# Layer one in a hand-written TensorE order: feed-forward products in quarter parts, attention steps as whole groups between them

## The chip, the cores and the metric

The kernel runs on one core of a Trainium2 chip. The metric is the device time of one launch in microseconds (us); lower is better. A core has five engines with a queue of their own: TensorE (PE, matrix products; PEld is its weight load), VectorE (DVE), ScalarE (ACT), GpSimd (POOL) and SyncE (SP, which issues DMA transfers). They meet only at semaphores.

## The reference

Windowed attention (each position sees itself and the 63 before it), then two feed-forward layers, all in float32:

```python
# q, k, v: (4, 8, 576, 64), window 64
scores = scale * np.matmul(q, k.transpose(0, 1, 3, 2))
scores = np.where(mask, scores, -1000000000.0)
scores = scores - np.max(scores, axis=-1, keepdims=True)
attn = np.exp(scores)
attn = attn / (np.sum(attn, axis=-1, keepdims=True) + 1e-09)
attn_out = np.matmul(attn, v)
x = attn_out.transpose(0, 2, 1, 3).reshape(2304, 512)
# layer one: w_in (512, 2048), w_out (2048, 512)
h = x @ w_in; r = np.maximum(h, 0.0); g = r * r; y1 = g @ w_out
# layer two: same sizes, elu
h = y1 @ w_in2; g = np.where(h > 0.0, h, np.exp(np.minimum(h, 0.0)) - 1.0)
y2 = g @ w_out2
```

## The kernel before

**Products.** A feed-forward product is made of three matmuls on pairs of a rounded high part and a low remainder: high by high, high by low, low by high (`mm3`, L454). A column tile of 512 tokens is one PSUM bank.

**Layer one.** The tokens are cut into blocks of 512, 256, 512, 512 and 512. Blocks t = 0, 1 and 2 run through the plain layer; blocks 3 and 4 meet it in another form, with combined weights (`stepw`, L692, from block 2's last steps on). A block has 16 steps j. A step makes one hidden tile: `m_h` issues 12 matmuls into the PSUM tile `ph` (4 chunks of the contraction by 3); ACT then makes relu and square into `g` and the high part of `gs`, DVE the low part. `m_out` multiplies `gs` into four accumulators o0 to o3 (4 by 3 matmuls; in a trace `o`). The loop issues h two steps ahead of o, and there are three buffers for `gs`. In block 0 `ph` has two banks, after that one.

**Attention.** A unit is one pair of heads for one block; the units of a block must be done before its h starts, so they are placed in the steps of the block ahead; those of blocks 3 and 4 (eight units, `pairs`) in block 2. A unit is

- `u_S` (L366): score matmuls, 64x128, two heads (a = 0, 1) on two halves of the array and in two PSUM banks; 16 of them for a block of 512, 8 for 256;
- softmax: per 128 columns one DVE maximum (`nm`, with the mask), one ACT exponential with its sum, a DVE normalisation in `pb`;
- `u_T` (L406): 8 transposes of `pb` through the identity, 4 to a PSUM bank, each bank copied by ACT to an SBUF tile `pt`;
- `u_PV` (L420): 16 matmuls of 64 columns on `pt` and the values; `u_X` copies the result (`xs`, or `xr` for the pairs, from which ACT makes `xo`).

`pa` is the PSUM tile of these, from three banks; `pt` shares its four SBUF buffers with `ev`, the copy of a finished accumulator that a DMA stores to `x2d`. `u_V2` does transposes and products of two units at once.

**What sets the order.** The program is written step by step, but inside layer one nothing pins the order on PE: a scheduler with a model of the engines places each instruction, and within a step's reach it takes h, o and attention matmuls as their inputs come. Two tools pin order: `slot` hangs background work (decoding and combining weights, with its ACT, DVE and DMA instructions: `top`, `tl`, `wo`, `y`) behind the last ACT and DVE instruction; and `in_turn`, used before only behind layer one, issues a function and chains its PE instructions (`last["pe"]`) behind the previous ones. It chains PE alone; ACT, DVE and SP stay with the scheduler, and each engine works its queue in order.

Of the kernel before, what the change touches and what calls it, by code (L numbers as in the profile page):

```python
# [19 lines left out]
P = 128  # L20
# [6 lines left out]
def window_attention_then_two_mlps(  # L27
# [86 lines left out]
    def split(hi, lo, x, eng):  # L114

        last["hi"] = act.activation(out=hi, in_=x, func=AF.Copy)
        last["lo"] = eng.tensor_tensor(out=lo, in0=x, in1=hi.bitcast(F32), op=ALU.subtract)
# [235 lines left out]
    def u_S(u, alloc):  # L353
        t, p = u
        qr, kr = raw[u]["q"], raw[u]["k"]
        m = BLOCKS[t] // P
        nm = at.tile([P, 2 * NQ], F32, tag="nm", name="nm")
        sm = at.tile([P, 2 * NQ], F32, tag="sm", name="sm")
        rc = at.tile([P, 2 * NQ], F32, tag="rc", name="rc")
        pss = [alloc() for _ in range(2)]  # L360
        for i in range(m):
            for a in range(2):
                d = slice(a * D, (a + 1) * D)
                for c in range(2):
                    o = (2 * i + c) * WIN
                    nc.tensor.matmul(  # L366
                        out=pss[a][c * WIN:(c + 1) * WIN, i * P:(i + 1) * P],
                        lhsT=qr[d, o:o + WIN], rhs=kr[d, o:o + P], start=True, stop=True,
                    )
        prb[u] = []  # L370
        for a0, heads in ((0, 1), (1, 1)) if m == NQ else ((0, 2),):
            w = heads * m
            pb = at.tile([P, 4 * P], F32, tag="pb", name="pb", bufs=4)
            for i in range(w):
                a, g = a0 + i // m, i % m
                b = a * m + g
                c, z = slice(i * P, (i + 1) * P), slice(g * P, (g + 1) * P)
                lead = [(T0[t] + (2 * g + h) * WIN) % S == 0 for h in range(2)]
                vec.tensor_tensor_reduce(
                    out=pb[:, c], in0=pss[a][:, z], in1=mask[1 + lead.index(True) if any(lead) else 0],  # L380
                    scale=-SCALE, scalar=3.0e38, op0=ALU.add, op1=ALU.min,
                    accum_out=nm[:, b:b + 1],
                )
                last["act"] = act.activation(
                    out=pb[:, c], in_=pb[:, c], func=AF.Exp,
                    bias=nm[:, b:b + 1], scale=-1.0, accum_out=sm[:, b:b + 1],
                )
            b0 = a0 * m
            r = rc[:, b0:b0 + w]
            vec.tensor_scalar(  # L390
                out=r, in0=sm[:, b0:b0 + w], scalar1=1.0e-9, scalar2=None, op0=ALU.add
            )
            vec.reciprocal(out=r, in_=r)
            x = pb[:, :w * P].rearrange("p (b x) -> p b x", x=P)
            last["dve"] = vec.tensor_tensor(
                out=x, in0=x, in1=r.unsqueeze(2).broadcast_to([P, w, P]), op=ALU.mult
            )
            prb[u].append((pb, w))

    def u_T(u, alloc):  # L400

        pts = []
        for pb, w in prb.pop(u):
            ps = alloc()
            for i in range(0, w * P, P):
                nc.tensor.transpose(out=ps[:, i:i + P], in_=pb[:, i:i + P], identity=ident)  # L406
            pt = at.tile([P, 512], F32, tag="pt", name="pt", bufs=4)
            copy(pt[:, :w * P], ps[:, :w * P], act)
            pts += [pt[:, i:i + P] for i in range(0, w * P, P)]
        return pts  # L410

    def u_PV(u, pts, alloc):
        t, p = u
        vr = raw.pop(u)["v"]
        ps = alloc()
        m = BLOCKS[t] // P
        for b in range(2 * m):
            for a in range(2):
                d = slice(a * D, (a + 1) * D)
                nc.tensor.matmul(  # L420
                    out=ps[d, b * WIN:(b + 1) * WIN], lhsT=vr[:, b % 2, b // 2, d],
                    rhs=pts[a * m + b // 2][:, (b % 2) * WIN:(b % 2 + 1) * WIN], start=True, stop=True,
                )
        return ps

    def u_X(u, ps):
        t, p = u
        n = BLOCKS[t]
        if t > TW:
            k = p // 2, t - TW - 1  # L430
            if k not in XQ:
                XQ[k] = xp.tile([P, CH, NMAX], F32, tag=f"xs{2 * k[0] + k[1]}", name="xr")
            copy(XQ[k][:, p % 2], ps[:, :n], vec if p % 2 else act)
            return
        s = xs[t, p] = xp.tile([P, 2, NMAX], F32R, tag=f"xs{p}", name="xs")
        split(s[:, 0, :n], s[:, 1, :n], ps[:, :n], vec)
# [1 line left out]
    def u_V(u, alloc):  # L438
        u_X(u, u_PV(u, u_T(u, alloc), alloc))

    def u_V2(us, alloc):

        pts = [u_T(u, alloc) for u in us]
        pss = [u_PV(u, x, alloc) for u, x in zip(us, pts)]
        for u, ps in zip(us, pss):
            u_X(u, ps)

    gs = {}
    acc = {}
# [5 lines left out]
                out=ps, lhsT=a[x], rhs=b[y], start=(first and i == 0), stop=(final and i == 2)  # L455
            )

    def m_h(t, j):
        n = BLOCKS[t]
        w = wt[j, 0]  # L460
        ps = h_alloc(t)
        for c in range(KD):
            x = xs[t, c]
            mm3(
                ps[:, :n],
                [w[:, r, c * P:(c + 1) * P] for r in range(2)],
                [x[:, r, :n] for r in range(2)],
                c == 0, c == KD - 1,
            )
        g = sc.tile([P, NMAX], F32, tag="g", name="g")  # L470
        s = sc.tile([P, 2, NMAX], F32R, tag="gs", name="gs", bufs=GB)
        act.activation(out=g[:, :n], in_=ps[:, :n], func=AF.Relu)
        act.activation(out=g[:, :n], in_=g[:, :n], func=AF.Square)
        split(s[:, 0, :n], s[:, 1, :n], g[:, :n], vec)
        gs[t, j] = s

    def m_out(t, j):
        n = BLOCKS[t]
        w = wt[j, 1]
        g = gs.pop((t, j))  # L480
        if j == 0:
            acc[0] = [ps_o.tile([P, 512], F32, tag=f"o{m}", name=f"o{m}") for m in range(KD)]
        for m, ps in enumerate(acc[0]):
            mm3(
                ps[:, :n],
                [w[:, r, m * P:(m + 1) * P] for r in range(2)],
                [g[:, r, :n] for r in range(2)],
                j == 0, j == NJ - 1,
            )
        if j == NJ - 1:  # L490
            leave1(t)

    def leave1(t):
        n = BLOCKS[t]
# [8 lines left out]
    def load_to(i):  # L503
        while nxt[0] <= min(i, len(order) - 1):
            u_load(order[nxt[0]])
            nxt[0] += 1
# [28 lines left out]
    def h_alloc(t):  # L535
        return among((0, 1) if t == 0 else (0,), "ph")
# [392 lines left out]
    lwx = ctx.enter_context(ExitStack())  # L929
    pairs = [(t, p) for t in range(TW + 1, NB) for p in range(HP)]  # L930
    for i, (t, j) in enumerate(its):
        if t == 0 and j > 2 and j % 2:
            m_out(t, j - 1)
            m_out(t, j)
        for n in ([i + LA] if t or j < 2 else [i + LA - 1, i + LA] if j % 2 else []):
            if n < len(its):
                m_h(*its[n])
        if t == 0 and j < 2:
            m_out(t, j)
        if (t, j) == (1, 0):  # L940
            late[0] = 1
        if (t, j) == (TW, 0):
            hw += [wts.tile([P, 2, NMAX], F32R, tag=f"w{k}", name="tl") for k in range(2)]
            more_lanes(0, 1)
        i0 = i - NJ * TW + 2
        if i0 in (2, 4, 6, 8):
            u_V2(pairs[i0 - 2:i0], a_alloc)
        if 0 <= i0 < len(pairs):
            u = pairs[i0]
            load_to(order.index(u) + 1)  # L950
            u_S(u, a_alloc)
        if t < TW:
            p, r = divmod(j, 3)
            u = (t + 1, p)
            if p < HP and r == 0:
                load_to(order.index(u) + 1)
                u_S(u, a_alloc)
            elif p < HP and r == 2 and p % 2:
                u_V2([(t + 1, p - 1), u], a_alloc)
        else:  # L960
            if j == 7:
                att.close()
                lw.append(pool(lwx, "lw", 1))
                w0_load(10)
            if j == 4:
                xw = x_make(-1, NMAX)
                next(xw)
            if j in (8, 9):
                next(xw)
            if j == 14:  # L970
                tl.update({k: lw[0].tile([P, NMAX], F32, tag=f"tl{k}", name="tl") for k in (1, 6, 7)})
            if j > 13:
                stepw(0, j - 13)
        if t:
            m_out(t, j)
        if t == 0:
            decode(min(LA + 3 + j, NU))
        slot(SLOTS.get((t, j), 0))
# [175 lines left out]
```

## Time and profile before

| | us |
|---|---|
| median of 3 runs (837.52 to 840.39) | 839.19 |
| profiled execution, its own time | 837.73 |
| its span in the trace | 836.0 |
| PE busy | 816.8 (98%) |
| DVE busy | 590.6 (71%) |
| ACT busy | 553.0 (66%) |
| mean granted PE clock | 0.996 |

1.7 us of the profiled execution lie outside its span. A row of the trace's timeline is a run of like instructions; its duration is that of the run with the pipeline's end, which overlaps the next row, so what a run cost PE is the distance from its start to the start of the next. The trace counts the float32 attention matmuls of 64 and 128 columns of `u_S` and `u_PV` twice: x32 there are 16 instructions. Stretches of the span by time: block 0's steps about 45 to 130 us, block 1's to 207, block 2's to about 315 (with the pairs' attention up to 284), combined steps from there on.

### The profile page before, as it was taken

What the parts mean: (1) busy time and instruction counts of PE and PEld (TensorE: products, weight loads), DVE (VectorE), ACT (ScalarE), POOL (GpSimd) and SP (SyncE); (2) the same over time, 40 slices, a digit from 0 to 9 for tenths busy, and PEclk for the clock granted to TensorE, in tenths of its full rate; (3) what the DMA queues carried; (4) which work ended last, traced back from release to release, by engine and by line L of the source; (5) the groups of instructions that cost most, each with busy time, mean ns of one, the idle gap of its engine ahead of it and who ended that gap; (6) DMA issues with size and microseconds to landing.
All of it is one profiled execution on the core that took longest, in us unless ns stands there. A gap on an engine that the chain in (4) does not pass through costs nothing.

```text
span 836.0 us, 14761 instructions
## 1 busy us (share of the span) xinstructions
PE 816.8 (98%) x5196; PEld 734.7 (88%) x5196; DVE 590.6 (71%) x1372; ACT 553.0 (66%) x1278; POOL 5.0 (1%) x23
## 2 busy tenths in 40 slices
PE   4899999999999999999999999999999999999998
PEld 3687788998777788888878899999999999999998
DVE  6898616877577857665675756698676798566875
ACT  5776536677777768777884557667477766477552
POOL 2000000000000000000000000000000000000000
PEclk9899999999999999999999999999999999999999
DMA  9996214556476498999969697878977876877832
GB/s 355 416 405 216 78 65 154 201 183 213 149 253 229 153 337 305 396 330 323 340 245 327 226 319 286 300 267 277 316 259 266 323 257 211 284 266 276 300 119 57
DMA packets 98681, 214.85 MB, mean 257 GB/s; under 512 B 26544, under 2 KB 53680, under 8 KB 90160
## 3 DMA queue, kind: packets, MB, share of 16 engines
q1 hardware_dynamic: 97776, 213.72, 72.8%
q8 instruction: 41, 0.67, 0.3%
q14 instruction: 32, 0.26, 0.1%
q10 hardware_dynamic: 832, 0.20, 0.1%
HBM read 160.41 MB, written 53.48 MB: 256 GB/s over the span
## 4 chain that ended last, share of the span: by engine, by line
PE 91%; ACT 5%; DMA 2%; DVE 1%; issue 1%; SPq 0%; ACTq 0%
PE o L454 23%; PE po L890 20%; PE px L692 14%; PE ph L454 12%; PE py L692 10%; PE po L692 6%; ACT pb L54 3%; PE pa L420 2%; PE pa L366 2%; PE pa L406 1%; PE px L890 1%; DMA tl<-in_moe_w_in_dram 1%; DMA wd<-wo 0%; DMA wraw<-in_moe_w_in_dram 0%; ACT top L54 0%
## 5 line engine op out<-in xcount | busy, mean ns | idle before, releaser
L454 PE MATMUL o<-gs,w 128*128 128x512 f32 (+1 forms) x960 | 216.4, 372 | 0.8 <-ACT gs L54 0.7
L454 PEld LDWEIGHTS o<-gs,w 128*128 128x128 f32 x960 | 167.1, 188 | 33.9 <-issue 2.2
L890 PE MATMUL po<-g,wr 128*128 128x384 f32 (+1 forms) x972 | 168.6, 333 | 0.0
L890 PEld LDWEIGHTS po<-g,wr 128*128 128x128 f32 x972 | 167.5, 188 | 0.0
L454 PE MATMUL ph<-xs,w 128*128 128x512 f32 (+1 forms) x576 | 126.0, 362 | 1.9 <-ACT xs L54 1.7
L54 ACT ACTIVATE g<-gr 128x384 fp32r<-128x384 f32 x168 | 86.9, 524 | 55.5 <-PE po L890 49.1
L454 PEld LDWEIGHTS ph<-xs,w 128*128 128x128 f32 x576 | 94.9, 189 | 19.2 <-ACT xs L54 2.6
L54 DVE TENSOR_TENSOR g<-gr,g 128x384 fp32r<-128x384 f32 x168 | 89.9, 552 | 16.1 <-ACT g L54 15.1
L692 PE MATMUL px<-xo,wr 128*128 128x384 f32 x432 | 83.8, 334 | 0.0
L692 PEld LDWEIGHTS px<-xo,wr 128*128 128x128 f32 x432 | 75.8, 188 | 0.3
L54 DVE TENSOR_TENSOR gs<-g,gs 128x512 fp32r<-128x512 f32 (+1 forms) x64 | 39.8, 622 | 42.1 <-ACT gs L54 41.6
L54 ACT ACTIVATE pb<-pb,nm 128x128 f32<-128x128 f32 x144 | 55.8, 389 | 14.9 <-DVE nm L54 14.9
L54 ACT ACTIVATE sy<-px 128x384 f32<-128x384 f32 x69 | 33.8, 490 | 41.7 <-PE px L692 41.3
L692 PE MATMUL po<-xo,wr 128*128 128x384 f32 x288 | 56.2, 334 | 0.0
L692 PE MATMUL py<-xo,wr 128*128 128x384 f32 x288 | 55.7, 334 | 0.0
L54 ACT ACTIVATE g<-ph 128x512 f32<-128x512 f32 (+1 forms) x48 | 24.9, 518 | 45.0 <-PE ph L454 44.9
L54 DVE TENSOR_TENSOR gr<-gr 128x384 f32<-128x384 f32 x96 | 52.2, 553 | 0.5
L54 DVE TENSOR_TENSOR gr<-sy,py 128x384 f32<-128x384 f32 x48 | 26.6, 554 | 35.1 <-PE py L692 23.3
L692 PEld LDWEIGHTS po<-xo,wr 128*128 128x128 f32 x288 | 50.5, 188 | 0.0
L692 PEld LDWEIGHTS py<-xo,wr 128*128 128x128 f32 x288 | 50.5, 188 | 0.0
L692 PE MATMUL px<-xo,w 128*128 128x512 f32 x192 | 46.4, 389 | 0.0
L54 DVE TENSOR_TENSOR wo<-y,wo 128x256 fp32r<-128x256 f32 (+1 forms) x65 | 32.2, 508 | 19.3 <-ACT wo L54 18.5
(88 smaller groups left out, 1098.1 us busy)
## 6 DMA issues: line engine op xcount, KB each, us to landing
wr<-wd SPq DMA_DIRECT2D x66, 1024.0 KB, 6.4
wd<-wo SPq DMA_DIRECT2D x38, 512.0 KB, 4.9
wr<-wd SPq DMA_DIRECT2D x24, 768.0 KB, 5.0
w<-wd SPq DMA_DIRECT2D x56, 256.0 KB, 5.6
vr<-in_v_dram SPq DMA_DIRECT2D x16, 512.0 KB, 5.6
wraw<-in_moe_w_in_dram SPq DMA_DIRECT2D x16, 511.8 KB, 8.7
wraw<-in_moe_w_out_dram SPq DMA_DIRECT2D x16, 511.8 KB, 9.8
wd<-tl SPq DMA_DIRECT2D x15, 512.0 KB, 4.6
```

The lines of the kernel that those rows point to most:

```text
L54: r = fn(*a, **kw)
L366: nc.tensor.matmul(out=pss[a][c * WIN:(c + 1) * WIN, i * P:(i + 1) * P], lhsT=qr[d, o:o + WIN], rhs=kr[d, o:o + P], start=True, stop=True,)
L406: nc.tensor.transpose(out=ps[:, i:i + P], in_=pb[:, i:i + P], identity=ident)
L420: nc.tensor.matmul(out=ps[d, b * WIN:(b + 1) * WIN], lhsT=vr[:, b % 2, b // 2, d], rhs=pts[a * m + b // 2][:, (b % 2) * WIN:(b % 2 + 1) * ...
L454: last["pe"] = nc.tensor.matmul(out=ps, lhsT=a[x], rhs=b[y], start=(first and i == 0), stop=(final and i == 2))
L692: last["pe"] = nc.tensor.matmul(out=ps[:, :NH], lhsT=w[:, wr_, c * P:(c + 1) * P], rhs=x[:, xr_, c], start=first and n == 0, stop=final an ...
L890: last["pe"] = nc.tensor.matmul(out=ps[m][:, lo:hi], lhsT=w[:, y, m * P:(m + 1) * P], rhs=s[:, x, lo:hi], start=k in fresh and p == 0 and ...
```

## The change

`m_h` and `m_out` become lists of four parts of three matmuls each (`parts_h`: one per chunk c; `parts_out`: one per accumulator m). Scores and the halves of `u_V2` (now `parts_V`: transposes of one unit, transposes of the other, products of one, products of the other) become items `between`. `mesh` puts each item ahead of an equal share of the step's parts, and issues all of it through `in_turn`, so that PE keeps the order as written: within a step h, then o. The score matmuls, the transposes and the products now set `last["pe"]`. In block 1 the scores move from j = 0, 3, 6, 9 to 0, 2, 6, 8. Of the pairs, an even score is put behind its step (`after_`) and the odd one at the front of the next step. For t = 1 and 2, o is now issued ahead of the step's other work.

```diff
@@ u_S
-                    nc.tensor.matmul(
+                    last["pe"] = nc.tensor.matmul(
@@ u_V2
-    def u_V2(us, alloc):
-        pts = [u_T(u, alloc) for u in us]
-        pss = [u_PV(u, x, alloc) for u, x in zip(us, pts)]
-        for u, ps in zip(us, pss):
-            u_X(u, ps)
+    def parts_V(us, alloc):
+        pts = {}
+        def turn(u):
+            pts[u] = u_T(u, alloc)
+        def close(u):
+            u_X(u, u_PV(u, pts.pop(u), alloc))
+        return [(f, u) for f in (turn, close) for u in us]
@@ m_h, m_out
-    def m_h(t, j):
+    def parts_h(t, j):
...
+        def piece(c):
...
+        return [(piece, c) for c in range(KD)]
...
-    def m_out(t, j):
+    def parts_out(t, j):
...
+        return [(piece, m) for m in range(KD)]
+
+    def mesh(fill, between):
+        if between:
+            gap = len(fill) // len(between)
+            fill = [x for k, b in enumerate(between) for x in [b] + fill[k * gap:(k + 1) * gap]] + fill[len(between) * gap:]
+        for f, a in fill:
+            in_turn(f, a)
@@ the loop over steps
+        fill, between, after_ = [], [], []
         if t == 0 and j > 2 and j % 2:
-            m_out(t, j - 1)
-            m_out(t, j)
+            fill += parts_out(t, j - 1) + parts_out(t, j)
...
-                m_h(*its[n])
+                fill += parts_h(*its[n])
+        if t or j < 2:
+            fill += parts_out(t, j)
...
         if t < TW:
-            p, r = divmod(j, 3)
-            u = (t + 1, p)
-            if p < HP and r == 0:
-                load_to(order.index(u) + 1)
-                u_S(u, a_alloc)
-            elif p < HP and r == 2 and p % 2:
-                u_V2([(t + 1, p - 1), u], a_alloc)
+            u = {x: (t + 1, p) for p, x in enumerate(((0, 3, 6, 9), (0, 2, 6, 8))[t])}.get(j)
+            ready_ = {5: 0, 11: 2}.get(j)
+            if ready_ is not None:
+                between += parts_V([(t + 1, ready_ + r) for r in range(2)], a_alloc)
+            if u:
+                between.append((score, u))
+        if i0 in (2, 4, 6, 8):
+            between += parts_V(pairs[i0 - 2:i0], a_alloc)
+        if 0 <= i0 < len(pairs):
+            (between if i0 < 2 or i0 % 2 else after_).append((score, pairs[i0]))
+        mesh(fill, between)
+        mesh(after_, [])
...
-        if t:
-            m_out(t, j)
```

Three places show what this makes of the queues. L454 of before is L458 of after; 128x256 are block 1's columns, 128x512 those of blocks 0 and 2.

PE in block 1, at the transposes and products of its first two units, before:

```order
L406 MATMUL pa<-ident,pb 128x128 x4
L454 MATMUL ph<-xs,w 128x256 x12
L406 MATMUL pa<-ident,pb 128x128 x4
L420 MATMUL pa<-pt,vr 64x64 x14
L454 MATMUL o_1500<-gs,w 128x256
L454 MATMUL o_1501<-gs,w 128x256
L454 MATMUL o_1502<-gs,w 128x256
L454 MATMUL o_1503<-gs,w 128x256
L420 MATMUL pa<-pt,vr 64x64
L454 MATMUL ph<-xs,w 128x256 x12
```

And the same place after:

```order
L406 MATMUL pa<-ident,pb 128x128 x8
L458 MATMUL ph<-xs,w 128x256 x6
L406 MATMUL pa<-ident,pb 128x128 x8
L458 MATMUL ph<-xs,w 128x256 x6
L420 MATMUL pa<-pt,vr 64x64 x16
L458 MATMUL o_1500<-gs,w 128x256 x3
L458 MATMUL o_1501<-gs,w 128x256 x3
L420 MATMUL pa<-pt,vr 64x64 x16
L458 MATMUL o_1502<-gs,w 128x256 x3
L458 MATMUL o_1503<-gs,w 128x256 x3
```

Transposes in fours and products in broken groups have become groups of 8 and 16, one unit each, with half an h or half an o between two.

PE in block 2, from the end of one pair's products through the next pair's scores, before (o_2631 to o_2634 are block 2's accumulators):

```order
L420 MATMUL pa<-pt,vr 64x64 x15
L366 MATMUL pa<-kr,qd 64x128 x16
L454 MATMUL ph<-xs,w 128x512 x2
L454 MATMUL o_2631<-gs,w 128x512 x2
L366 MATMUL pa<-kr,qd 64x128 x8
L454 MATMUL o_2631<-gs,w 128x512
L454 MATMUL o_2632<-gs,w 128x512 x3
L454 MATMUL o_2633<-gs,w 128x512 x2
L366 MATMUL pa<-kr,qd 64x128 x8
L454 MATMUL o_2633<-gs,w 128x512
```

And after (the accumulators are o_2562 to o_2565 there):

```order
L420 MATMUL pa<-pt,vr 64x64 x16
L458 MATMUL o_2564<-gs,w 128x512 x3
L458 MATMUL o_2565<-gs,w 128x512 x3
L366 MATMUL pa<-kr,qd 64x128 x32
L458 MATMUL ph<-xs,w 128x512 x12
L458 MATMUL o_2562<-gs,w 128x512 x3
```

The first score of a pair was whole and the second in two halves, each between products; now both stand in one row of 32 with a whole h behind them.

PE where block 1 ends, before (o_1501 to o_1503 are block 1's last products, o_2631 and on block 2's first):

```order
L454 MATMUL ph<-xs,w 128x512 x12
L454 MATMUL o_1501<-gs,w 128x256 x2
L454 MATMUL o_1502<-gs,w 128x256 x3
L454 MATMUL o_1503<-gs,w 128x256 x3
L406 MATMUL pa<-ident,pb 128x128 x8
L454 MATMUL o_2631<-gs,w 128x512 x3
L406 MATMUL pa<-ident,pb 128x128 x4
L454 MATMUL o_2632<-gs,w 128x512 x3
L454 MATMUL ph<-xs,w 128x512 x12
L454 MATMUL o_2633<-gs,w 128x512 x3
L454 MATMUL o_2634<-gs,w 128x512 x3
L406 MATMUL pa<-ident,pb 128x128 x4
```

And after:

```order
L458 MATMUL ph<-xs,w 128x512 x12
L458 MATMUL o_1500<-gs,w 128x256 x3
L458 MATMUL o_1501<-gs,w 128x256 x3
L458 MATMUL o_1502<-gs,w 128x256 x3
L458 MATMUL o_1503<-gs,w 128x256 x3
L406 MATMUL pa<-ident,pb 128x128 x8
L458 MATMUL ph<-xs,w 128x512 x6
L406 MATMUL pa<-ident,pb 128x128 x8
L458 MATMUL ph<-xs,w 128x512 x6
L420 MATMUL pa<-pt,vr 64x64 x16
L458 MATMUL o_2562<-gs,w 128x512 x3
L458 MATMUL o_2563<-gs,w 128x512 x3
```

The second unit's transposes stood behind 18 products of block 2, and the last four of them behind a whole h; now six matmuls of h stand between the two units' groups.

Over the whole of layer one PE has 834 such rows in place of 1005. The transposes of block 2's units, in block 1's steps, fall into 4 groups (9 before) and those of the pairs into 8 (14); the products into 4 (8) and 8 (7), and those in block 0's steps into 4 (3); the scores into 4 (11) for block 2's units and 5 (12) for the pairs, whose first two stand in block 1's last steps. The two heads alternate through the whole score in 8 of these 12 scores; in one of block 2's units and in the second score of three of the four pairs, one head's 8 come first and then the other's.

ACT's queue at the second pair, between the pair's exponentials and the copies of its transposes, before (`xo` belongs to the pair before, `top`, `wo` and `tl` to the combined weights):

```order
L54 ACTIVATE pb,sm<-pb,nm 128x128 x7
L54 ACTIVATE gs<-g 128x512
L54 ACTIVATE pb,sm<-pb,nm 128x128
L54 ACTIVATE top<-tl 128x256
L54 ACTIVATE wo<-y 128x2x256
L54 ACTIVATE g<-ph 128x512
L54 ACTIVATE top<-top 128x256
L54 ACTIVATE pt<-pa 128x512
```

And after:

```order
L54 ACTIVATE pb,sm<-pb,nm 128x128 x8
L54 ACTIVATE g<-ph 128x512
L54 ACTIVATE xo<-xr 128x1024
L54 ACTIVATE top<-tl 128x256
L54 ACTIVATE wo<-y 128x2x256
L54 ACTIVATE top<-top 128x256
L54 ACTIVATE g<-g 128x512
L54 ACTIVATE pt<-pa 128x512 x3
```

`xo` has moved from the midst of the exponentials behind them, and a relu's square now stands ahead of three copies.

## Rows read from the trace of the kernel before

**Rows 1.** The page's first part: busy time and share of each engine.

```profile
PE 816.8 (98%) x5196; PEld 734.7 (88%) x5196; DVE 590.6 (71%) x1372; ACT 553.0 (66%) x1278; POOL 5.0 (1%) x23
```

**Rows 2.** Waits of PE: who for whom: total us, times, longest us.

```profile
PE pa L420 <- ACT pt L54: 2.5, 3, 1.7
```

**Rows 3.** Busy time by stretch: span, PE, PEld, DVE, ACT, POOL, clock, DMA share, GB/s.

```profile
140.00:200.00 60.00, 60.00 (x631) 55.21 (x626) 48.36 (x156) 42.10 (x139) 0.00 (x0) 1.00 0.56 186
200.00:284.00 84.00, 82.78 (x787) 66.79 (x786) 59.60 (x220) 66.10 (x204) 0.00 (x0) 1.00 0.63 216
...
315.00:420.00 105.00, 105.00 (x465) 86.95 (x464) 69.10 (x149) 81.35 (x175) 0.00 (x0) 1.00 0.95 341
```

**Rows 4.** Timeline of PE in block 0: start us, us, engine, line, operation, count.

```profile
107.93 2.88 PE L454 MATMUL o<-gs,w 128*128 128x512 f32 x12
110.65 2.89 PE L454 MATMUL ph<-xs,w 128*128 128x512 f32 x12
113.38 1.04 PE L406 MATMUL pa<-ident,pb 128*128 128x128 f32 x8
114.17 3.00 PE L454 MATMUL o<-gs,w 128*128 128x512 f32 x12
117.00 1.97 PE L454 MATMUL ph<-xs,w 128*128 128x512 f32 x8
118.91 1.15 PE L420 MATMUL pa<-pt,vr 128*64 128x64 f32 x32
119.99 3.02 PE L454 MATMUL o<-gs,w 128*128 128x512 f32 x12
122.84 3.79 PE L454 MATMUL ph<-xs,w 128*128 128x512 f32 x16
```

**Rows 5.** Timeline of PE in block 1: scores' first and last piece, half products.

```profile
126.56 1.08 PE L366 MATMUL pa<-kr,qd 64*64 64x128 f32 x14
...
160.16 0.69 PE L420 MATMUL pa<-pt,vr 128*64 128x64 f32 x16
160.77 1.69 PE L454 MATMUL ph<-xs,w 128*128 128x256 f32 x12
...
175.09 0.44 PE L366 MATMUL pa<-kr,qd 64*64 64x128 f32 x4
```

**Rows 6.** Timeline of PE in block 2: two pairs' first score, the later one's second.

```profile
218.11 1.10 PE L366 MATMUL pa<-kr,qd 64*64 64x128 f32 x32
...
240.05 1.10 PE L366 MATMUL pa<-kr,qd 64*64 64x128 f32 x32
241.08 0.50 PE L454 MATMUL ph<-xs,w 128*128 128x512 f32 x1
...
242.66 1.09 PE L366 MATMUL pa<-kr,qd 64*64 64x128 f32 x16
243.69 1.21 PE L454 MATMUL o<-gs,w 128*128 128x512 f32 x4
244.83 1.09 PE L366 MATMUL pa<-kr,qd 64*64 64x128 f32 x16
```

**Rows 7.** Timeline of ACT; in brackets idle time before and its releaser.

```profile
147.19 0.36 ACT L54 ACTIVATE g<-ph 128x256 f32<-128x256 f32 x1
...
210.05 0.60 ACT L54 ACTIVATE pt<-pa 128x512 f32<-128x512 f32 x1 [1.35 <-DMA x2d<-ev]
...
242.78 1.04 ACT L54 ACTIVATE xo<-xr 128x1024 fp32r<-128x1024 f32 x1
244.12 0.39 ACT L54 ACTIVATE pb<-pb,nm 128x128 f32<-128x128 f32 x1
```

**Rows 8.** Timeline of DVE: low part of `gs`, and one maximum of a score.

```profile
110.08 0.69 DVE L54 TENSOR_TENSOR gs<-g,gs 128x512 fp32r<-128x512 f32 x1 [3.75 <-ACT gs L54]
...
241.19 0.29 DVE L54 CUSTOM_DVE_ANT_0 pb<-pa,mask 128x128 f32<-128x128 f32 x1
```

**Rows 9.** The tile `ev` between 200 and 225 us: issue to landing.

```profile
DMA to landing us min/median/max: 2.7/3.8/4.7
```

More of the change, by code (lines that the diff above doesn't have):

```diff
@@ L405, in u_T @@
             for i in range(0, w * P, P):
-                nc.tensor.transpose(out=ps[:, i:i + P], in_=pb[:, i:i + P], identity=ident)
+                last["pe"] = nc.tensor.transpose(out=ps[:, i:i + P], in_=pb[:, i:i + P], identity=ident)
             pt = at.tile([P, 512], F32, tag="pt", name="pt", bufs=4)
@@ L419, in u_PV @@
                 d = slice(a * D, (a + 1) * D)
-                nc.tensor.matmul(
+                last["pe"] = nc.tensor.matmul(
                     out=ps[d, b * WIN:(b + 1) * WIN], lhsT=vr[:, b % 2, b // 2, d],
@@ L456, in mm3 @@
             )
-    def m_h(t, j):
+    def parts_h(t, j):
         n = BLOCKS[t]
[L460 to L463, printed above, removed]
+        ps = []
+        def piece(c):
+            if c == 0:
+                ps.append(h_alloc(t))
+            w, x = wt[j, 0], xs[t, c]
             mm3(
-                ps[:, :n],
+                ps[0][:, :n],
                 [w[:, r, c * P:(c + 1) * P] for r in range(2)],
@@ L469, in m_h, with piece @@
             )
[L470 to L475, printed above, removed]
-    def m_out(t, j):
-        n = BLOCKS[t]
[L479 to L483, printed above, removed]
+            if c < KD - 1:
+                return
+            g = sc.tile([P, NMAX], F32, tag="g", name="g")
+            s = sc.tile([P, 2, NMAX], F32R, tag="gs", name="gs", bufs=GB)
+            act.activation(out=g[:, :n], in_=ps[0][:, :n], func=AF.Relu)
+            act.activation(out=g[:, :n], in_=g[:, :n], func=AF.Square)
+            split(s[:, 0, :n], s[:, 1, :n], g[:, :n], vec)
+            gs[t, j] = s
+        return [(piece, c) for c in range(KD)]
+    def m_h(t, j):
+        for f, c in parts_h(t, j):
+            f(c)
+    def parts_out(t, j):
+        n = BLOCKS[t]
+        def piece(m):
+            w, g = wt[j, 1], gs[t, j]
+            if j == 0 and m == 0:
+                acc[0] = [ps_o.tile([P, 512], F32, tag=f"o{k}", name=f"o{k}") for k in range(KD)]
             mm3(
-                ps[:, :n],
+                acc[0][m][:, :n],
                 [w[:, r, m * P:(m + 1) * P] for r in range(2)],
@@ L489, in m_out @@
             )
-        if j == NJ - 1:
-            leave1(t)
+            if m == KD - 1:
+                gs.pop((t, j))
+                if j == NJ - 1:
+                    leave1(t)
+        return [(piece, m) for m in range(KD)]
[5 more added lines that the diff above has]
+            in_turn(f, a)
     def leave1(t):
@@ L931, in window_attention_then_two_mlps @@
     for i, (t, j) in enumerate(its):
+        fill, between, after_ = [], [], []
         if t == 0 and j > 2 and j % 2:
-            m_out(t, j - 1)
-            m_out(t, j)
+            fill += parts_out(t, j - 1) + parts_out(t, j)
         for n in ([i + LA] if t or j < 2 else [i + LA - 1, i + LA] if j % 2 else []):
             if n < len(its):
-                m_h(*its[n])
-        if t == 0 and j < 2:
-            m_out(t, j)
+                fill += parts_h(*its[n])
+        if t or j < 2:
+            fill += parts_out(t, j)
         if (t, j) == (1, 0):
@@ L944, in window_attention_then_two_mlps, with score @@
             more_lanes(0, 1)
[L945 to L949, printed above, removed]
+        def score(u):
             load_to(order.index(u) + 1)
             u_S(u, a_alloc)
+        i0 = i - NJ * TW + 2
         if t < TW:
-            p, r = divmod(j, 3)
-            u = (t + 1, p)
-            if p < HP and r == 0:
-                load_to(order.index(u) + 1)
-                u_S(u, a_alloc)
-            elif p < HP and r == 2 and p % 2:
-                u_V2([(t + 1, p - 1), u], a_alloc)
-        else:
+            u = {x: (t + 1, p) for p, x in enumerate(((0, 3, 6, 9), (0, 2, 6, 8))[t])}.get(j)
[10 more added lines that the diff above has]
+        mesh(after_, [])
+        if t == TW:
             if j == 7:
@@ L973, in window_attention_then_two_mlps @@
                 stepw(0, j - 13)
-        if t:
-            m_out(t, j)
         if t == 0:
```

## The prediction

> **What bounds the kernel now.** I read the engines' shares first: PE is busy for 816.8 of 836.0 us, DVE and ACT for 71% and 66% [rows 1]. So PE's queue sets the end, and an edit can gain only by making its matmuls shorter, by taking away what one kind of matmul costs behind another, or by removing idle time. The stretches come second. From 140 to 200 us PE has no idle time, and from 200 to 284 us it lacks 1.22 us [rows 3]; in the list of waits the largest entry that falls into layer one is products that wait for ACT's copies of transposes, 2.5 us in three times [rows 2]. In that stretch ACT is busy for 66.1 of 84 us [rows 3]: not the bound, but the engine with least to spare. Third, PE's timeline, read from start to start, which shows what a switch costs.
>
> A plain run of 12 matmuls of 512 columns takes 2.72 us (107.93 to 110.65), 0.227 each. The run of 12 behind the transposes takes 2.83 (114.17 to 117.00), the 8 ahead of a unit's products 1.91 where 8 by 0.227 make 1.81, and the 12 behind them 2.85 [rows 4]. So an attention group costs 0.11 us beside itself if it is transposes, and 0.10 + 0.13 = 0.23 if it is products. For scores: 4 matmuls between two groups take 1.14 (243.69 to 244.83) where 0.91 would do: 0.23 again [rows 6].
>
> The scores hold the larger surprise. A whole score of 16 matmuls takes 1.03 us (240.05 to 241.08), and half a score, 8 matmuls, takes as long (242.66 to 243.69) [rows 6]. In the whole one the two heads alternate, on two halves of the array; in the half one a single head's 8 stand alone. Splitting a score by heads doubles its price.
>
> **The change, part by part.** The sum goes against the profiled execution's 837.73 us; its median stands 1.46 us above that, and I carry the difference over.
>
> *Scores whole, not split.* Block 2's four scores lie in 11 pieces from 126.56 to 175.09 [rows 5], whose own times, start to start, add to 7.3 us. After, three are whole and one in halves by head: 3 x 1.03 + 2.05 = 5.1. Gain 2.2. Of the pairs, the first score becomes whole (0.35 gained); the second ones of three pairs stay in halves, so nothing is gained inside these.
>
> *Score groups joined.* 11 groups become 4, and 12 become 5: 14 groups fewer at 0.22: gain 3.1.
>
> *Products of attention.* Half a unit's products take 0.61 us (160.16 to 160.77) [rows 5], a whole unit's 1.08 [rows 4]; a group more costs 0.61 x 2 + 0.23 - 1.08, about 0.35. Block 1's steps have 4 groups fewer, block 0's one more, the pairs one more of which the parts were unequal (taken at nothing, 0.35 at most): gain 1.0.
>
> *Transposes.* 5 and 6 groups fewer at up to 0.11: between 0 and 1.2; since some switches are now between transposes and products with no feed-forward run between, I take 0.5.
>
> *Idle time that goes.* The 1.22 us of block 2's stretch [rows 3] were waits of an order that is no more: gain 1.2, and the new order's waits are charged below.
>
> Gains together: 2.2 + 0.35 + 3.1 + 1.0 + 0.5 + 1.2 = 8.35, between 6 and 9.
>
> The costs are waits that a fixed order brings. PE waits in place where the scheduler would have put something else, and all that is queued behind a waiting matmul on PE waits with it: h, o and the combined steps after them.
>
> *Block 0's start.* o now stands strictly behind h. The low part of `gs` lands 2.84 us after h's end (110.77 against 107.93) [rows 4, 8], which o's second matmul, 2.72 + 0.23 = 2.95 later, just meets. I take 0, with -0.25 to +0.5.
>
> *Block 0 to 1.* Two h of block 1 stand one behind the other on the one bank of `ph`. The second waits for the relu that empties it: 0.36 us [rows 7] and 0.19 until it begins, 0.55.
>
> *Block 1 to 2.* The accumulators' copies `ev` share their buffers with `pt`. Already before, ACT waited 1.35 us there for stores [rows 7], which take 2.7 to 4.7 us to land [rows 9]; PE had products of block 2 and a whole h to run meanwhile. Now the first unit's transposes stand right behind block 1's last product, six matmuls (1.4 us) later the second's, whose last bank waits for a copy that waits for a store. Of a median landing of 3.8 us, 1.4 + 0.8 are covered: a wait of 1.5 (0.8 to 2.5).
>
> *Second scores of three pairs.* They stand right behind the first; a half that writes a bank just filled waits for DVE's maxima of it, 4 at 0.21 [rows 8]. Of 0.85 us, the 1.03 of the half itself covers part: 0.3 each, 0.9 (0 to 2).
>
> *ACT's queue in the pairs.* A pair's 16 exponentials at 0.39 [rows 7] take 6.2 us. Counted from the end of the first score, PE runs the second (2.05), h (to 5.1), o (to 7.9), the first unit's transposes (8.7), half an h (10.1), the second's, half an h (12.2), and then wants the first unit's `pt`. ACT has behind the exponentials a relu, in the second pair also `xo` of 1.04 [rows 7], three items of the combined weights and a square ahead of the `pt` copies: these begin near 10.6 and free the bank for the second unit's transposes some 0.65 us late. In the other pairs a copy stands ahead of the square and is in time. With 0.3 for a relu that is late in block 1, I take 1.0 (0 to 4: for the upper end each of the four pairs loses about that 1.04 once).
>
> Costs together: 0 + 0.55 + 1.5 + 0.9 + 1.0 = 4.0, between 1.4 and 9.
>
> Nothing else is on the path: the same weights are loaded by SP, whose queue nothing on PE's order blocks; from 315 to 420 us the DMA share is 0.95 with PE busy for all 105.00 us [rows 3], so a transfer there has kept pace, and a start 4 us earlier leaves it that much less lead. I charge nothing for that, and price it as a rival.
>
> Net: 837.73 - 8.35 + 4.0 = 833.4 for an execution like the profiled one, and 834.9 for the median. I forecast **835.0**.
>
> *A rule against the edge prices.* The rows show 0.11 us behind transposes, which run on the whole array as the feed-forward products do [rows 4]. The Trainium skill, "TensorEngine Tiling (Array Packing)", Tiling Modes, Key Properties, says that the engine is drained when the tiling mode changes. By that the scores' and products' edges have their reason, and the trace agrees with 0.23; transposes would be free, and the gain 0.5 lower, 835.4. The row decides.
>
> **The rivals.** *First, gains given back (about the same time as before).* The pairs' attention now goes through in fewer PE matmuls: before, a pair took 22 us (218.11 to 240.05, between two first scores) [rows 6], after it takes some 18 by my walk. ACT's share of work for a pair is the same, so what was 66.1 of 84 us [rows 3] becomes 66.1 in about 70. For it: the 2.5 us that PE already waited for `pt` [rows 2] came with more room than this. Against it: ACT's background items could fall back behind without holding PE, as the scheduler puts some of them there. If each of the four pairs gives back 1 us, the time is 839. The Trainium skill, "TensorE: Matmul & The Clock Gate", Part 2, Step-by-step, says that matmuls stay in program order, so that a waiting one is not stepped over; no row of before shows it.
>
> *Second, slower.* The place is the `pt` copies in the four pairs and at block 2's start: PSUM banks that hold transposes come free only through ACT. If the 16 exponentials do not run without gaps (each needs DVE's maximum, which shares its queue with low parts and combined weights), the copies start 3 us later than in my walk. Four pairs at 3 us, less the 1.0 already charged, with the first store wait at 2.5: 835.0 + 12 - 1.0 + 1.0 = 847 at full size; it decides from the point at which a pair loses more than about 2 us, where 4 x 2 eats all of the net gain and more (835.0 + 8 - 1 = 842). The Trainium skill, "TensorEngine Tiling (Array Packing)", PSUM Bottleneck, warns that copies from PSUM become the bound once TensorE is faster. No row here shows that; ACT's 66 of 84 [rows 3] is what comes nearest.
>
> *Third, the gain goes to the DMA-bound stretch* behind layer one: PE arrives 4 us earlier at 315 us and waits for weights, as a share of 0.95 allows [rows 3]. Then 838 to 839. Against it, not a single wait of PE is there now. *Fourth, the change does not do what it says*: on PE it does, by the order shown, except for four scores in halves, which is in the sum.
>
> **How the numbers follow.** My forecast of a gain (831 to 836.7) has 0.58, the first and third rivals together 0.28 (837 to 841), the second 0.14. A measurement of this kernel can tell 0.3%, 2.5 us, from no change: faster is under 836.7, slower over 841.7. Faster 0.58, the same 0.28, slower 0.14. The lower end is all gains with the least costs, 839.2 - 9 + 1.4 = 831.6, rounded to 831; the upper end, 6 gained and 9 lost, is 842.2, of which I keep 841.5: it leaves the second rival outside.
>
> **What would show it.** Scores as runs of x16 or x32 and 14 switches fewer show the first two terms; a score that costs 1.03 when whole confirms the largest. Idle brackets on PE are to be expected at block 1's first h (released by ACT's `g`), at block 2's first transposes (ACT `pt`, and on ACT the store of `ev`), and at three second scores (DVE). The combined steps should begin some 4 us earlier. The forecast is wrong if the pairs' `pt` copies show brackets of over 1 us on PE in each pair, if PE idles after 315 us, or if an edge costs nothing where groups are whole, in which case less was to be had than I count.

## The result and the profile after

The changed kernel takes 843.98 us (median of 10 runs, 841.9 to 848.72), the kernel before 838.88 (10 runs): a ratio of 1.007 with a 95% interval of 1.0047 to 1.0093 (of the two medians 1.006). It is slower by 5.1 us; 835.0 was forecast, with 841.5 as the upper end. The profiled execution takes 843.65 us, 5.9 more than that of before.

The page's first part of the kernel after, and the stretch of block 2's attention (columns as in [rows 3]):

```profile
PE 814.7 (97%) x5196; PEld 733.2 (87%) x5196; DVE 589.5 (70%) x1372; ACT 555.0 (66%) x1278; POOL 5.0 (1%) x23
```

```profile
200.00:284.00 84.00, 77.31 (x758) 62.46 (x757) 60.91 (x221) 64.38 (x200) 0.00 (x0) 0.98 0.63 213
```

PE is busy 2.1 us less than in [rows 1] although the span is 5.9 longer: matmuls got cheaper, and waits came. From 200 to 284 us PE lacks 6.69 us where it lacked 1.22 [rows 3], and the granted clock is 0.98 where it was 1.00. PE's waits in this stretch (who for whom: total us, times, longest) add to these 6.69 us:

```profile
PE pa L366 <- DVE nm L54: 5.4, 3, 3.1
PE ph L458 <- ACT g L54: 0.9, 2, 0.6
PE pa L406 <- ACT pt L54: 0.4, 1, 0.4
```

The kernel before has two in the same stretch, which make its 1.22 us:

```profile
PE o L454 <- ACT gs L54: 0.7, 1, 0.7
PE pa L420 <- ACT pt L54: 0.5, 1, 0.5
```

So the first entry of the changed kernel is new: second scores that wait for DVE's maxima of the first. PE's timeline shows two of the three (of the four pairs, three have their scores in block 2's steps; these three are counted here and in the experiments as first, second and third):

```profile
236.15 1.96 PE L366 MATMUL pa<-kr,qd 64*64 64x128 f32 x48
241.21 1.57 PE L366 MATMUL pa<-kr,qd 64*64 64x128 f32 x16 [3.09 <-DVE nm L54]
242.71 4.13 PE L458 MATMUL ph<-xs,w 128*128 128x512 f32 x12
...
259.38 1.96 PE L366 MATMUL pa<-kr,qd 64*64 64x128 f32 x48
263.36 1.09 PE L366 MATMUL pa<-kr,qd 64*64 64x128 f32 x16 [2.01 <-DVE nm L54]
```

The first 24 matmuls of a pair's 32 (x48: counted twice) run at once. The last 8, which write a bank that the first score filled, wait 3.09 and 2.01 us in the second and third pair; in the first it is 0.25, with the maxima at 0.21 each started at once. Behind the long wait the matmuls themselves are slow: the second half takes 1.50 us in place of 1.02, the next 12 of h 3.96 (242.71 to 246.67) in place of 2.86. The granted clock of three stretches says why:

```profile
236.00:241.00 5.00, 2.12 (x49) 1.72 (x48) 1.81 (x11) 1.50 (x6) 0.00 (x0) 1.00 0.77 265
241.00:243.00 2.00, 1.79 (x17) 1.49 (x18) 2.00 (x20) 2.00 (x12) 0.00 (x0) 0.67 1.00 312
243.00:247.00 4.00, 4.00 (x14) 3.16 (x14) 3.97 (x18) 4.00 (x18) 0.00 (x0) 0.74 0.84 301
```

After the pause PE was granted its lower level, 1.2 GHz, for a part of the last two stretches and the full 2.4 GHz again later: 0.48 + 1.10 = 1.6 us on top of the wait.

What DVE was doing meanwhile stands in its own timeline, and what it waited for in ACT's:

```profile
235.06 0.68 DVE L54 COPY xr<-pa 128x512 f32<-128x512 f32 x1
239.19 0.69 DVE L54 TENSOR_TENSOR wo<-y,wo 128x512 fp32r<-128x512 f32 x1 [3.45 <-ACT wo L54]
239.80 0.28 DVE L54 CUSTOM_DVE_ANT_0 pb<-pa,mask 128x128 f32<-128x128 f32 x1
```

```profile
238.53 0.63 ACT L54 ACTIVATE wo<-y 128x512 fp32r<-128x512 f32 x1 [4.11 <-DMA wd<-wo]
...
261.01 0.63 ACT L54 ACTIVATE wo<-y 128x512 fp32r<-128x512 f32 x1 [2.84 <-DMA wd<-wo]
```

The chain, from its end: PE waits for the maxima; the maxima stand in DVE's queue behind `wo<-y,wo`, the low part of a combined weight, which has nothing to do with attention; that waits for ACT's high part; ACT waits for its staging tile `wo`, whose last contents a DMA is still storing to `wd`. DVE was free from 235.7 to 239.2 us.

Where the 6 us were lost can be bounded from both sides. The first combined product begins at 321.23 us:

```profile
320.55 0.84 PE L458 MATMUL o<-gs,w 128*128 128x512 f32 x3
321.23 0.62 PE L717 MATMUL px<-xo,w 128*128 128x512 f32 x2
```

In the kernel before it begins at 315.15, so 6.08 us are lost ahead of it, and nothing of note behind it. I set time against products done (0.2267 us for each matmul of 512 columns, half for 256) at the end of each group of attention products. By this account the change stands against before at +2.8 us at the end of block 0, then -2.4 over block 1's steps up to its last unit, +0.2 over the boundary, and +0.4, +3.3 and +1.8 over the next three pairs; together +6.1.

Of the 2.8 us, 1.5 belong to this execution and not to the change: they are there already at 39 us, ahead of the first score of block 0's steps. PE's granted clock was at its lower level (0.51) shortly before, where it was full in the trace of before (the changed kernel first):

```profile
30.00:33.50 3.50, 3.50 (x11) 2.85 (x11) 3.34 (x7) 2.49 (x3) 0.00 (x0) 0.51 1.02 411
```

```profile
29.80:34.00 4.20, 4.20 (x48) 3.24 (x46) 4.04 (x7) 3.29 (x4) 0.00 (x0) 1.00 1.02 404
```

Eight matmuls of h that begin in it take 3.42 us here and 2.00 in before. The runs below with only block 2 and with only block 1 fixed have the same in their traces, the others not. What is left, 1.2, is the order of block 0: from that point to the end of the block's attention, the eight traces with the fixed order spend 12.3 to 12.4 us beside products, the six with the order of before 11.2.

### The profile page after: what moved, and what is told of

Same layout as the page of the kernel before. It is cut to its first block, busy times and chain, and to the rows that moved or that the text cites. A ratio compares the mean times of both kernels' runs of the same rounds, so it can differ in the third digit from the quotient of the medians.

```text
span 841.9 us, 14760 instructions
## 1 busy us (share of the span) xinstructions
PE 814.7 (97%) x5196; PEld 733.2 (87%) x5196; DVE 589.5 (70%) x1372; ACT 555.0 (66%) x1278; POOL 5.0 (1%) x23
## 4 chain that ended last, share of the span: by engine, by line
PE 78%; ACT 7%; DVE 5%; DMA 4%; issue 1%; ACTq 0%; DVEq 0%
PE po L915 20%; PE o L458 18%; PE px L717 12%; PE ph L458 9%; PE py L717 9%; PE po L717 6%; ACT pb L54 2%; DMA wd<-wo 2%; DVE y L54 2%; ACT g L54 2%; DMA tl<-in_moe_w_out_dram 1%; PE pa L420 1%; PE pa L406 1%; PE px L915 1%; ACT top L54 1%
## 5 line engine op out<-in xcount | busy, mean ns | idle before, releaser
L458 PE MATMUL o<-gs,w 128*128 128x512 f32 (+1 forms) x960 | 212.2, 371 | 0.6 <-DVE gs L54 0.2
L458 PEld LDWEIGHTS o<-gs,w 128*128 128x128 f32 x960 | 166.8, 188 | 33.4 <-DVE gs L54 2.2
L458 PE MATMUL ph<-xs,w 128*128 128x512 f32 (+1 forms) x576 | 126.3, 367 | 5.0 <-ACT g L54 2.6
L458 PEld LDWEIGHTS ph<-xs,w 128*128 128x128 f32 x576 | 96.4, 192 | 24.4 <-ACT g L54 4.5
```

The source lines that it names most:

```text
L458: last["pe"] = nc.tensor.matmul(out=ps, lhsT=a[x], rhs=b[y], start=(first and i == 0), stop=(final and i == 2))
```

## The experiments

Theory A: the loss is made in block 2, where PE may no longer pass a second score that waits behind background work in DVE's and ACT's queues. Rival B: the fixed order of blocks 0 and 1 costs it. Rival C: the exponentials and maxima alone are too slow for a shorter pair. Rival D: DVE's own work holds the bank, not the store.

**Block 2 or blocks 0 and 1.** The blocks in `FREE` are issued as in the kernel before and not chained (for them scores and attention steps are called in place); the other blocks keep the change.

```diff
+    FREE = (2,)
...
-        mesh(fill, between)
-        mesh(after_, [])
+        if t not in FREE:
+            mesh(fill, between)
+            mesh(after_, [])
```

> Block 2 back to the scheduler's order; blocks 0 and 1 keep the fixed one. Theory A (the loss is made in block 2: PE waits in a pair's second score for DVE's maxima, which stand behind a background product that waits for a store): the trace of the changed kernel loses 5.7 us in the three pairs, so about 838.3 (837 to 840), with no bracket over 1 us on a score. Theory B (the fixed order of blocks 0 and 1 costs it, their start above all, 1.5 to 2.5 us later there): 842 or more.

> Blocks 0 and 1 back to the scheduler's order; block 2 keeps the fixed one. Theory A: the whole loss stays, 844 to 845, since block 1's gain of some 2 us goes as well. Theory B: 839 to 841.

With block 2 free: 838.89 against 838.25 of before, ratio 1.0006 (0.9992 to 1.0019); the wait on second scores shrinks to one of 0.9. With only block 2 fixed (`FREE = (0, 1)`): 847.99, ratio 1.0107 (1.0088 to 1.0127), with PE's list headed as in the changed kernel:

```profile
PE pa L366 <- DVE nm L54: 5.6, 3, 3.3
```

Theory A holds against B: all of the loss needs block 2's order. The second result is 3 us above its expectation, and not all of that is explained: its trace (an execution of 845.49 us) has a wait of 1.04 us at block 2's first transposes that the changed kernel does not have, and the low clock ahead of block 0, 1.5 us against before. The expectation of the first run took the 1.5 to 2.5 us at the start for the order's; the larger part was that clock.

**The second score later.** The odd score moves from ahead of h to between h and o.

```diff
-            (between if i0 < 2 or i0 % 2 else after_).append((score, pairs[i0]))
+            if i0 > 2 and i0 % 2:
+                fill[4:4] = [(score, pairs[i0])]
+            else:
+                (between if i0 < 2 else after_).append((score, pairs[i0]))
```

> The changed kernel with a pair's second score between h and o in place of ahead of h. Theory A: 12 matmuls of h, 2.9 us, run while DVE is held, so of the waits of 0.25, 3.09 and 2.01 us 0.2 stay, and the clock does not fall behind them (1.6 us): 837 to 838. Theory C (ACT's queue as such is the bound, since a pair's 16 exponentials now have 18 us in place of 22): the wait moves to the second unit's transposes or the products, 842 to 845.

Missed: 843.08, ratio 1.0058 (1.0036 to 1.0081). No score waits any more; PE's timeline shows who does now:

```profile
226.96 0.63 PE L406 MATMUL pa<-ident,pb 128*128 128x128 f32 x4 [1.18 <-DVE rc L54]
...
248.24 0.63 PE L406 MATMUL pa<-ident,pb 128*128 128x128 f32 x4 [1.84 <-DVE rc L54]
...
267.11 0.63 PE L406 MATMUL pa<-ident,pb 128*128 128x128 f32 x4 [1.72 <-ACT g L54]
271.32 0.63 PE L406 MATMUL pa<-ident,pb 128*128 128x128 f32 x4 [2.20 <-ACT pb L54]
```

By their releasers, the delay of DVE and ACT went through the softmax to the transposes. Covering one wait does not help when what is late is the queue behind it. This fits C as well as A, so the queue's contents had to be changed.

**The store's buffer.** In block 2's first steps the staging tile alternates between two places; before, only every third combined weight went to the second.

```diff
-            if n % 3 == 0 and hw:
+            if hw and n % (3 if lw else 2) == 0:
```

> The changed kernel with the combined weights' staging tile alternating between two buffers in block 2's first steps (before every third in the other one). Theory A: ACT's wait for the store of the tile before, 4.1 and 2.8 us, is gone or under 1; the second scores wait less than 0.5 each: 838 to 840. Theory D (DVE's own work, maxima and copies, is what holds the bank): the waits of 3 and 2 us stay, 843 to 845.

839.40, ratio 1.0014 (1.0001 to 1.0027): 4.6 us less than the changed kernel's median. ACT's waits for the store of `wo` between 200 and 284 us fall from 8.2 to 0.8. The long wait of the second pair is gone (236.50); one is left:

```profile
236.50 1.09 PE L366 MATMUL pa<-kr,qd 64*64 64x128 f32 x16 [0.25 <-DVE nm L54]
...
257.32 1.47 PE L366 MATMUL pa<-kr,qd 64*64 64x128 f32 x16 [2.29 <-DVE nm L54]
```

DVE's timeline there shows no wait for a store:

```profile
253.58 0.68 DVE L54 TENSOR_TENSOR gs<-g,gs 128x512 fp32r<-128x512 f32 x1
254.18 0.68 DVE L54 TENSOR_TENSOR wo<-y,wo 128x512 fp32r<-128x512 f32 x1
254.78 1.22 DVE L54 TENSOR_TENSOR xr<-xr 128x1024 f32<-128x1024 f32 x1
255.92 0.42 DVE L54 SCALAR_TENSOR_TENSOR y<-tl,top 128x256 uint32<-128x256 uint32 x1
256.25 0.28 DVE L54 CUSTOM_DVE_ANT_0 pb<-pa,mask 128x128 f32<-128x128 f32 x1
```

So the store made the 3.09, as A has it, but A's expectation of under 0.5 for each score was missed once: what stays in the third pair is D, DVE busy without a gap on other work ahead of the maxima (`gs` of the feed-forward product, `xr` of the pair before, `wo` and `y` of the background).

**No background at all.** The background work of block 2's first six steps is put off to its last ten; three runs, one otherwise as the change, and two with block 0 also back in the scheduler's order, of which the first has the second score later too.

```diff
-    SLOTS |= {(2, j): 3 for j in range(NJ)}
+    SLOTS |= {(2, j): 5 if j > 5 else 0 for j in range(NJ)}
```

> The changed kernel with the background work of block 2's first six steps put off to its last ten (5 slots each in place of 3). Theory A (background work that waits for DMA, ahead of the maxima in ACT's and DVE's queues): the second scores wait 0.25 us each, as the first of them does now, and the clock stays: 844.0 - 4.6 - 1.6 = 837.8 (836.5 to 839). Theory C (the exponentials and maxima alone are too slow for the shorter period): 1 to 2 us per pair stay on scores or transposes, 841 to 844.

The other two add these to it, the last one only the first line:

```diff
+    FREE = (0,)
...
+            if i0 > 2 and i0 % 2:
+                fill[4:4] = [(score, pairs[i0])]
```

> Blocks 1 and 2 fixed, background work put off as before, and a pair's second score between h and o. Theory A: with ACT and DVE free, h covers the maxima and the second scores alternate whole, 1.03 in place of 2.05 us three times: 837.8 - 3 - 1 for block 0 = 833 to 835. Theory C: the transposes wait for the exponentials, 1 to 2 us in each pair: 837 to 840.

> As the run before, but with the second score where the change puts it: theory A 836.5 (835.5 to 838); the distance to the run before is what whole second scores and the place between h and o bring, 2 to 3.5 us by theory A, none or less than none by theory C.

856.60, 860.32 and 858.84, ratios 1.0208 (1.0183 to 1.0234), 1.0247 (1.0227 to 1.0266) and 1.0227 (1.0204 to 1.0249): as times all three missed. Their traces still answer the question. In the first of them the second scores read

```profile
217.30 1.09 PE L366 MATMUL pa<-kr,qd 64*64 64x128 f32 x16 [0.26 <-DVE nm L54]
...
236.10 1.09 PE L366 MATMUL pa<-kr,qd 64*64 64x128 f32 x16 [0.26 <-DVE nm L54]
...
254.91 1.09 PE L366 MATMUL pa<-kr,qd 64*64 64x128 f32 x16 [0.25 <-DVE nm L54]
...
312.20 0.61 PE L717 MATMUL px<-xo,w 128*128 128x512 f32 x2
...
486.56 0.69 PE L717 MATMUL px<-xo,wr 128*128 128x384 f32 x1 [14.69 <-ACT xo L54]
```

With the queues clear, every second score waits a quarter of a microsecond, and layer one's end comes at 312.20: 9 us earlier than with the change (1.6 of them the clock ahead of block 0), 3 earlier than before. So C falls: exponentials and maxima alone fit the shorter pair. What followed at 486 us came with putting the work off. ACT's timeline ahead of it:

```profile
475.04 0.42 ACT L54 ACTIVATE wo<-y 128x256 fp32r<-128x256 f32 x1 [2.44 <-DMA wd<-wo]
...
478.86 0.72 ACT L54 ACTIVATE wo<-y 128x256 fp32r<-128x256 f32 x2 [0.53 <-DMA wd<-wo]
485.66 0.84 ACT L54 ACTIVATE xo<-xq 128x768 fp32r<-128x768 f32 x1 [6.09 <-DMA xq<-x2d]
```

The background work reaches into the combined steps, its stores are waited for, and the load of the next input lands late; that this load stood behind those stores in SP's queue fits, but was not tried. The second score's later place gave nothing here either: in the trace of the second of the three a second score takes 1.52 us, not the 1.03 of alternating heads, and each pair's transposes wait 0.24 to 0.25.

**Block 1 alone.**

```diff
-    FREE = (2,)
+    FREE = (0, 2)
```

> Fixed order in block 1 alone; blocks 0 and 2 by the scheduler. From the traces block 1's order gains 2.2 to 2.6 us and block 0's costs 1.0 to 1.4: 836 to 837. If block 0's cost in the trace is only a difference between two executions, 838.5, as with blocks 0 and 1 fixed.

841.46, ratio 1.0025 (1.0013 to 1.0037): missed, slower. Four waits of h for the relu (`ph <- ACT g`), 3.7 us, where the changed kernel has 1.7 in block 1. By the account above, block 1's order gains 2.4 us in each trace with blocks 0 and 1 fixed and block 1's background work as in the change, and costs 1.5 in the three with block 0 free. Which of the two it is hangs on when ACT comes to the relu, and nothing pins ACT's order; what about block 0 decides it was not tried.

**Buffers in the kernel before, and what could be faster.** The same edit of the staging tile in the kernel before; then in the changed kernel, once with the background of block 2's first six steps behind the second scores only (6 slots in the odd steps, none in the even ones; the first edit below), once with a third of it moved into block 1 (there 2 slots up to step 10, in block 2's first six steps 2 in place of 3; the second edit), both with the buffers kept; last in the first run's kernel.

```diff
-    SLOTS |= {(2, j): 3 for j in range(NJ)}
+    SLOTS |= {(2, j): 3 if j > 5 else 6 * (j % 2) for j in range(NJ)}
```

```diff
-    SLOTS |= {(1, j): 2 if j < 5 else 1 for j in range(NJ)}
-    SLOTS |= {(2, j): 3 for j in range(NJ)}
+    SLOTS |= {(1, j): 2 if j < 11 else 1 for j in range(NJ)}
+    SLOTS |= {(2, j): 3 if j > 5 else 2 for j in range(NJ)}
```

> The kernel before with the two staging buffers in turn of the fourth run. Theory A: ACT waits for stores there too (2.4 us in block 2), but PE has h and o to run meanwhile, so nothing: 838 to 839.5. If the buffers are a gain by themselves, 834 to 836, and the fourth run then says less of the change.

> The changed kernel with two staging buffers, and the background work of block 2's first six steps only in the odd ones, 6 slots in place of 3, behind the second score. Theory A: nothing stands ahead of the maxima that waits, second scores 0.25 each, 837 to 838.5; it may come back as waits for ACT's copies of transposes, then 839 to 842.

> The changed kernel with two staging buffers and 6 of the 18 background slots of block 2's first six steps moved ahead into block 1's steps. Theory A: the 2.29 us that the fourth run still waited in the third pair go, and 1.4 of lost clock with them: 835.5 to 837.5, faster than both. Theory C: block 1's relu waits grow by what is moved there, 838 to 840.

> Blocks 0 and 1 in the fixed order, block 2 by the scheduler (as in the first run), with the two staging buffers. If what block 1's order gains in the trace and what the buffers gain add up: 834.5 to 836, faster than the kernel before with the buffers (836.4). If the gain of block 1 is taken back in block 2, as the first run's time says, 836 to 838.

The kernel before with the buffers takes 836.41, ratio 0.9971 (0.9957 to 0.9985): a gain of 2.5 us, against my expectation of none. Its trace has no idle time on PE in block 2, where [rows 3] show 1.22 us, but it accounts for less than the gain: the first combined product begins 0.96 us earlier than before's, and 0.3 of that stands ahead of block 0. Nor are the stores out of ACT's way; PE has no wait beside this one:

```profile
267.31 0.63 ACT L54 ACTIVATE wo<-y 128x512 fp32r<-128x512 f32 x1 [3.00 <-DMA wd<-wo]
```

So why the buffers help the kernel before stays open. Of the 4.6 us that they save in the changed kernel, 2.5 they save without the fixed order too. The 2.1 that are left are within the three intervals (about 2.5 us together); that the buffers do something particular to the fixed order is shown by the trace, where the wait of 3.09 went, and not by the times. The other two versions missed: 841.47, ratio 1.0033 (1.0015 to 1.0052), with waits of 1.09 and 2.76 on second scores; and 843.07, ratio 1.004 (1.0025 to 1.0056), where the scores of two pairs wait 0.25 but an h in block 1's last steps waits 2.74 for ACT, which had waited 1.83 and 0.71 for loads of background work, the first transposes of block 2 wait 1.17, and the last pair's score 1.61. Each time the background work was moved, a fixed step of PE found it ahead of itself elsewhere. The last, block 2 free with the buffers, takes 836.67, ratio 0.998 (0.9966 to 0.9994), faster than before too and no different from the buffers alone: the fixed order of blocks 0 and 1 adds nothing that can be measured.

## Why the prediction was wrong

- **The failed step** is the cost "second scores of three pairs". It was sized at 0.9 us, 0 to 2, from four maxima at 0.21 [rows 8], as if DVE took them the moment they could start. Where that held, the wait was 0.25, as in the fifth run for all three. But DVE's queue had a background conversion ahead of the maxima, which waited for ACT, and ACT for a store: 5.4 us of waits and 1.6 of lower clock, 7.0 in place of 0.9. These 6.1 us are two thirds of the 9.4 between the gain forecast (4.3) and the loss measured (5.1); the rest is in the points below, block 1 above all.
- **What I could have read.** ACT's order showed the background items behind a pair's exponentials, and so ahead of the next pair's; and `wo` waits for its store in the kernel before as well, three times, 1.63 us at most. I walked ACT's queue item by item for the `pt` copies, but priced each item at its busy time. An item that can wait for a DMA has two prices, and in before PE, with h and o to run, shows no wait beside that of 1.63.
- **What I misread.** I took the 2.5 us of waits for `pt` [rows 2] as falling into layer one. Two of the three, 1.96 us, stand ahead of block 0's steps, at 17.42 and 29.51 us; the steps have one of 0.51, at 282.79. So what I held for the first rival was mostly not there. The ends of the sums are loose too: the costs' upper bounds add to 9.55, not 9, which would put the upper end at 842.8, still under 843.98.
- **Scores, groups, transposes.** Layer one with clear queues ended 3.0 us earlier than before (fifth run), waits of relu included, where my net was 4.3. So the gains were there, but 1.3 us smaller than the net. In block 1, 2.4 us were gained where 2.2 + 1.5 + 1.4 + 0.25, less 0.85 of waits, were foreseen: 4.5. The waits there were 1.69. The scores' own time fell by 2.7 (7.3 to 4.6: three at 1.03, one at 1.53), more than the 2.2 foreseen. That leaves 1.4 for the joined groups of scores, products and transposes, where 3.15 were foreseen: the price of a group was set about twice too high, and which of the three kinds it was, was not tried.
- **Block 0 to 1**: 0.55 foreseen, 0.47 measured at the second h. **Block 1's relu**: 0.3 foreseen, three more waits of 0.33, 0.73 and 0.16 measured. **Block 0**: taken at 0; its order costs 1.2, of which 0.35 was in the sum as a group more of products.
- **Block 1 to 2**: 1.5 foreseen through the shared `ev` and `pt` buffers; in the changed kernel 0.61, and for relu, not for a store. **`pt` copies in the second pair of the four** (the first in block 2's steps): 0.65 foreseen, 0.42 measured.
- **The rivals.** The slower one had the right engine and the right stretch (ACT's queue in block 2's pairs) and a time of 842 to 847, and 843.98 falls into it. But its place was wrong: not copies of transposes, which waited 0.42, but maxima behind a weight's store; and exponentials with gaps were not the cause, as the fifth run shows. It had 0.14; that its time came true is in part luck, since another mechanism made it. The third rival, waits behind 315 us, did not come.
- **The two rules.** Transposes among feed-forward products still cost 0.08 (six matmuls of h take 0.80 us, from 157.71 to 158.51, between two groups, where 6 of 256 columns take 0.72 in a plain run), so they are not free, as the rows had said. The Trainium skill, "TensorEngine Tiling (Array Packing)", Key Properties, names a change of tiling mode as what drains the engine; these transposes keep the mode (128*128 in the timeline), so it gives no reason for the 0.08. The Trainium skill, "TensorEngine Tiling (Array Packing)", PSUM Bottleneck, says that copies from PSUM may become the bottleneck after tiling has sped TensorE up. The second scores agree with that in form, since PE waits for DVE to read a bank; but DVE had been idle for 3.45 us just before, so it was not the reader's speed.

## What to carry to other kernels

A fixed order on one engine takes away its freedom to pass a late input, so waits of the engines that feed it, hidden until then, come onto the path; go through the queues of those engines with the longest wait of each item, DMA waits and background work above all, and not with its busy time. If the feeding queues stay with a scheduler, moving work about in them can shift the wait rather than end it, as in three runs here. A second buffer for the tile that the background work stores from took most of the loss away.

## What the runs showed that was not expected

A pause of 3.09 us on PE was followed by a lower granted clock (0.67 and 0.74 on average over the next 2 and 4 us), which cost 1.6 us more than the pause; a pause of 2.01 (263.36) was followed by a half score of 1.02 and full speed. In the run with two buffers a pause of 2.29 was followed by a half of 1.40 in place of 1.02, and by h in 4.05 in place of 2.86. The low clock ahead of block 0, 1.5 us in three of the fourteen traces, is as large as several terms of the prediction, so two traces are better compared stage by stage than by their ends. And in the kernel before, a second buffer for a background store was worth 2.5 us, of which PE's waits there show 1.22.
